# A gated recurrence and a soft mixture of experts on one core: the ninth token group as rows of seven tokens, with scans by halves of the time

## The chip, the cores and the metric

The kernel runs on one core of a Trainium2 chip. The core has five engines that run beside each other, each in the order of its own instruction list: TensorE (PE, with its weight loads shown as PEld), VectorE (DVE), ScalarE (ACT), GpSimd (POOL) and SyncE (SP, which here only issues transfers). Sixteen DMA engines move data between HBM and the core's memory. The metric is the device time of one execution in microseconds (us). PSUM is the memory that PE writes; a tile there holds its buffer until its last reader is done.

## The reference

The inputs are x and f_logit of 4 batches x 5056 steps x 256 channels in float32, a lower bound per channel, and the weights of 8 experts with 4 slots each. First a recurrence runs over the steps, then a soft mixture of experts over all 20224 tokens:

```python
f = lower_bound + (1.0 - lower_bound) * sigmoid(f_logit)
for t in range(S):
    h = f[:, t] * h + (1.0 - f[:, t]) * x[:, t]
    y[:, t] = h
logits = y @ phi                            # 20224 x 32
d = softmax of logits over the tokens;  c = softmax of logits over the slots
slot_out[e] = relu(slot_input[e] @ w1[e]) @ w2[e]     # slot_input = d.T @ y
out = c @ slot_out
```

No slot's output is known before every token has been through the recurrence, so the kernel reads all inputs first and writes all outputs last.

## The kernel before

**Tiling.** The 5056 steps of a batch are cut into ten groups. Groups 0 to 7 and 9 have 512 steps, group 8, the ninth, has the remaining 448 (`odd`, line 55). A unit is one group of one batch, so there are 40; units 32 to 35 are the ninth group of batches 0 to 3, units 36 to 39 the last group. The main loop (from line 499) runs over the units and works ahead: at unit n it loads units n+6, gates n+3 or n+4, multiplies n+3, transposes n+1 and n+2, scans n and takes n-1 on. The order of the calls in this loop is the order of instructions on each engine; nothing is reordered later, so an instruction that waits holds up all that stand behind it on its engine.

**Stages of a unit.**
- `load` (lines 215 to 236) issues the transfers of f_logit and x on SP, into tiles f_t and x_t of two units, three buffers each. Units 8 to 31 (`long`, line 198) come eight tokens a row, 8 KB; units 0 to 7 and 36 to 39 four tokens a row. The ninth group takes three DMAs for each pair of units and each of f_logit and x (lines 227 and 231): three tokens a row for 384 steps of each batch, and the last 64 steps of both batches together, one token on each partition.
- `gate` (line 246): ACT's sigmoid, s_t, for a pair of units.
- `enter` (line 257): POOL multiplies s_t and x_t to u_t.
- `s_to_channels` and `u_to_channels`: PE transposes s_t and u_t to channels by steps, into the PSUM tiles sp (one buffer, a pair of units) and up (two buffers). The ninth group (lines 266 and 269) needs one transposition for the shared last 64 steps and three more for each unit; the long units transpose 64 partitions at a time (line 282).
- `decay` (lines 310 and 317): ACT makes the decays a from sp, two instructions for a pair of units.
- `scan` (line 328): DVE runs the recurrence along the free axis, one instruction for each half of the channels, started from the last column of the batch's group before.
- `to_tokens` (line 341): PE transposes h back to tokens by channels into hp, a PSUM tile with a single buffer; `keep_tokens` (line 358) copies it to ht, by DVE for even units and by ACT for odd ones among the last.
- `logits`, `exps` (line 381, ACT), `weights_to_tokens` (lines 393 and 396, PE and a DVE copy to et) and `slots` (line 423, PE) take a whole group or two on.
- `idle` (line 194) issues matrix products whose result nobody reads, at chosen units; `BETWEEN` places some inside a transposition of units 8 and 12.

**Weights.** POOL issues 16 weight loads between its multiplications (`W_AT`, line 167; lines 147 and 157): six of them after `enter` of the last unit. The last two experts' w2 go to a tile w_t.

**The end.** The slots' experts run from line 615; PE's last products with w_t (line 714) lead to slot_out (line 749), and the output products (lines 778 and 815) and 21 MB of output follow.

The ninth group's order around its scans, for the steps below: at unit n the loop issues (decay or load), `enter`, `to_tokens(n-1)`, `s_to_channels` of the next pair at even n, `u_to_channels(n+1)`, idle products, then `scan(n)`, then `keep_tokens(n-1)`. At unit 35 the gate of 38/39 and the exp of groups 6 and 7 stand behind the decays of 36/37.

## Time and profile before

| | |
|---|---|
| median of 3 runs | 196.72 us (196.70 to 196.83) |
| the profiled execution | 196.81 us, span 195.0 us |
| mean granted PE clock over the span | 0.877 |
| busy: PE, DVE, ACT, POOL | 155.0, 147.5, 139.6, 104.8 us |
| HBM read, written | 58.23 MB, 20.71 MB |

The span is from the first instruction's start to the last one's end; the profiled execution's own time is 1.81 us longer. A line of the timeline gives the start, the duration, the engine, the source line, the operation, what is written and read with shapes, how many instructions, and in brackets how long the engine sat idle before it and what ended that. "L328" is line 328 of the kernel before. A granted clock of 1.00 is PE's full speed. The DMA share is the mean busy share of the 16 DMA engines; packets overlap, so it can come out over 1.

### The profile page before, as it was taken

Reading aid. Unit: us, or ns where it says so; the run is one execution under the profiler, and the core shown is the slowest. Engines: PE = TensorE matmul, PEld = TensorE weight load, DVE = VectorE, ACT = ScalarE, POOL = GpSimd, SP = SyncE. Lnnn points to the kernel's source line nnn. Section 1 sums busy time; section 2 is a strip of 40 time slices with the busy share of each in tenths; the row PEclk is TensorE's granted clock in tenths of the full one; section 3 lists DMA queues with packets and bytes.
Section 4 is the critical chain, followed back from the end, with each engine's and each line's share of the span. In section 5 each row is a group of like instructions: output and inputs, shape, how many; then the busy total and the mean of one; then the engine's idle time right before and its main releaser. Section 6 shows DMA issues by size and latency. Waiting matters only on the chain.

```text
span 195.0 us, 3288 instructions
## 1 busy us (share of the span) xinstructions
PE 155.0 (79%) x1206; PEld 105.7 (54%) x1206; DVE 147.5 (76%) x192; ACT 139.6 (72%) x200; POOL 104.8 (54%) x82
## 2 busy tenths in 40 slices
PE   4868888999989989788897887999899999990000
PEld 4446665776777767566675756567674433220000
DVE  2679797899799999999999999634199798770000
ACT  3688688799789999999998595634269987771000
POOL 2589568874997779884979969485030000000000
PEclk9999999999999999999999999999995555555555
DMA  6999999999999999999999999999949999999995
GB/s 202 417 423 419 428 422 427 430 423 359 381 423 425 414 323 423 430 417 317 392 422 395 273 232 213 214 213 214 184 165 426 426 440 430 430 430 430 430 430 218
DMA packets 14433, 70.75 MB, mean 363 GB/s; under 512 B 1601, under 2 KB 2882, under 8 KB 10450
## 3 DMA queue, kind: packets, MB, share of 16 engines
q1 hardware_dynamic: 11504, 62.13, 77.0%
q0 software_dynamic: 2912, 8.42, 21.8%
q8 instruction: 9, 0.15, 0.3%
q14 instruction: 6, 0.05, 0.1%
q10 hardware_dynamic: 2, 0.00, 0.0%
HBM read 58.23 MB, written 20.71 MB: 405 GB/s over the span
## 4 chain that ended last, share of the span: by engine, by line
DMA 30%; PE 21%; DVE 18%; ACT 9%; issue 6%; POOL 5%; ACTq 0%; SPq 0%; POOLq 0%; DVEq 0%
DMA x_t<-in_x_dram 15%; DVE h L328 14%; PE op L815 10%; DMA w_t<-in_moe_w_dram 9%; DMA w_sb<-in_moe_w_dram 6%; POOL u_t L257 4%; ACT oc L820 3%; DVE ht L358 3%; PE hp L341 3%; PE up L282 2%; ACT a L310 2%; PE op L778 2%; PE sp L272 2%; ACT s_t L246 1%; ACT ob L772 1%
## 5 line engine op out<-in xcount | busy, mean ns | idle before, releaser
L257 POOL TENSOR_TENSOR u_t<-s_t,x_t 128x1024 bf16<-128x1024 bf16 (+1 forms) x39 | 82.4, 2129 | 22.2 <-ACT s_t L246 14.0
L328 DVE TENSOR_TENSOR_SCAN h<-a,h,up 128x512 bf16<-128x512 f32 (+1 forms) x72 | 86.6, 1251 | 4.8 <-PE up L282 3.5
L246 ACT ACTIVATE s_t<-f_t 128x2048 bf16<-128x2048 f32 (+2 forms) x23 | 38.3, 1668 | 7.2 <-DMA f_t<-in_f_logit_dram 4.9
L341 PE MATMUL hp<-base,h 128*128 128x128 f32 (+1 forms) x160 | 28.9, 303 | 9.6 <-DVE ht L358 6.7
L341 PEld LDWEIGHTS hp<-base,h 128*128 128x128 f32 (+1 forms) x160 | 22.3, 207 | 19.4 <-DVE ht L358 11.6
L815 PE MATMUL op<-slot_bd,etall 64*128 64x512 bf16 x62 | 25.9, 582 | 0.9 <-DVE ob L768 0.2
L310 ACT ACTIVATE a<-sp,lbs 128x1024 f32<-128x1024 bf16 x24 | 25.4, 1115 | 0.6 <-PE sp L272 0.6
L820 ACT ACTIVATE oc<-op,rrow 128x256 f32<-128x256 f32 x54 | 22.1, 488 | 4.5 <-PE op L815 4.3
L823 DVE TENSOR_TENSOR oc<-op,rrow 128x512 f32<-128x512 f32 x35 | 22.3, 684 | 3.0 <-PE op L815 2.9
L194 PE MATMUL slot_ps<-base 128*128 128x256 f32 x74 | 22.7, 418 | 0.0
L272 PE MATMUL sp<-base,s_t 128*128 128x128 f32 x144 | 20.2, 281 | 3.0 <-ACT a L317 2.0
L317 ACT ACTIVATE a<-sp,lbs 128x512 f32<-128x512 bf16 (+2 forms) x22 | 17.8, 858 | 3.8 <-PE sp L272 3.5
L272 PEld LDWEIGHTS sp<-base,s_t 128*128 128x128 f32 x144 | 16.3, 144 | 6.1 <-ACT a L317 3.8
L282 PE MATMUL up<-base,u_t 64*128 64x64 f32 x192 | 17.8, 230 | 1.3 <-POOL u_t L257 1.0
L815 PEld LDWEIGHTS <-etall 64*128 64x128 bf16 x62 | 9.1, 152 | 16.6 <-issue 11.8
L282 PEld LDWEIGHTS up<-base,u_t 64*128 64x128 f32 x192 | 14.0, 138 | 6.1 <-POOL u_t L257 2.7
L358 DVE COPY ht<-hp 128x512 f32<-128x512 f32 (+1 forms) x22 | 14.7, 666 | 0.8 <-PE hp L341 0.8
L358 ACT COPY ht<-hp 128x512 f32<-128x512 f32 (+1 forms) x18 | 10.4, 580 | 6.6 <-PE hp L341 6.4
L194 PEld LDWEIGHTS slot_ps<-base 128*128 128x128 f32 x74 | 12.9, 201 | 2.5 <-issue 1.1
L328 DVE TENSOR_TENSOR_SCAN h<-a,up 128x512 bf16<-128x512 f32 x8 | 9.4, 1211 | 1.9 <-PE up L272 1.8
L372 PE MATMUL lg<-h,phi 128*32 128x512 bf16 (+1 forms) x80 | 9.6, 389 | 0.0
L272 PE MATMUL up<-base,u_t 128*128 128x128 f32 x48 | 7.9, 287 | 1.1 <-POOL u_t L257 1.0
(124 smaller groups left out, 150.4 us busy)
## 6 DMA issues: line engine op xcount, KB each, us to landing
f_t<-in_f_logit_dram SPq DMA_DIRECT2D x12, 1024.0 KB, 12.5
x_t<-in_x_dram SPq DMA_DIRECT2D x12, 1024.0 KB, 11.7
out_dram<-oc SPq DMA_DIRECT2D x6, 2048.0 KB, 13.2
w_sb<-in_moe_w_dram POOLq DMA_DIRECT2D x14, 512.0 KB, 11.1
f_t<-in_f_logit_dram SPq DMA_DIRECT2D x12, 512.0 KB, 8.4
x_t<-in_x_dram SPq DMA_DIRECT2D x12, 512.0 KB, 9.9
out_dram<-ob SPq DMA_DIRECT2D x1, 2048.0 KB, 10.1
out_dram<-oc SPq DMA_DIRECT2D x2, 896.0 KB, 6.9
```

Of the source, the lines that this page charges most:

```text
L194: nc.tensor.matmul(slot_bank[:, 1], ident_f, wide_ident, start=False, stop=False, skip_group_check=True)
L246: nc.scalar.activation(s_t, f_t, ACT.Sigmoid, scale=-1.0)
L257: nc.gpsimd.tensor_tensor(uts[n][:, :r], s_t[:, :r], x_t[:, :r], ALU.mult)
L272: nc.tensor.transpose(ps[:, :, r], t[:, r], ident_f)
L282: nc.tensor.transpose(v[:, :, r], t(r)[k].bitcast(F32), ident_f[k, k])
L310: nc.scalar.activation(a, sp[:, :, :, :, o], ACT.Identity, scale=nomlb[:, ds(o, 1)], bias=1.0)
L328: nc.vector.tensor_tensor_scan(h[:, :T, o], decays[n // 2, o][:, n % 2, :T], up[:, :T, o], hs[number(g - 1, b)][:, ds(used(g - 1) - 1, 1), ...
L341: nc.tensor.transpose(hp[:n_p, r], hw[:, :n_p, r], ident_f)
L358: copy(hts[g][:n_p, b].rearrange("p r d -> p (r d)").bitcast(F32), hps.pop(n)[:n_p].rearrange("p r c -> p (r c)"))
L815: nc.tensor.matmul(op.rearrange("p u d -> p (u d)"), ew[:, :, r], slot_bd[ds(j * 2 * NS, 2 * NS)].rearrange("s u d -> s (u d)"), start=Tru ...
L820: nc.scalar.activation(ob[:, u, r], op[:, u], ACT.Copy, scale=scale[:, r, ds(u, 1)])
L823: nc.vector.tensor_tensor(ob[:, :, r], op, scale[:, r].unsqueeze(2).broadcast_to([P, 2, D]), ALU.mult)
```

## The change

The ninth group is read as rows of seven tokens. One DMA for a pair of units and each of f_logit and x puts step 7p+r of the pair's first batch on partition 2p and of its second batch on partition 2p+1. The seven columns of a pair lie one after the other in the tile, as before four in the first unit's part and three in the second's. A unit of this group is now not a batch but a half of the time: the even unit of a pair covers steps 0 to 223 of both batches, the odd one steps 224 to 447. So `u_to_channels` takes partitions 0 to 63 or 64 to 127 of both units' u_t, seven transpositions of 64 partitions; `s_to_channels` takes seven of 128 partitions for a pair; `scan` runs four instructions of 224 columns, for two batches and two halves of the channels. Tokens of both batches follow after the odd unit's scans, and all four copies to ht are ACT's. Idle products go at units 11, 15, 17 and 36 (two there), and one of the two inside unit 12's transposition.

```diff
+    R7 = R + R3
@@ load
-                    nc.sync.dma_start(
-                        out=t[:, 0, R3],
-                        in_=src[ds(b, 2), ds(t0 + P * R3, L)].rearrange("b t d -> t b d"))
-                    for m in range(2):
-                        nc.sync.dma_start(
-                            out=t[:, m, ds(0, R3)],
-                            in_=src[b + m, ds(t0, P * R3)].rearrange("(p r) d -> p r d", r=R3))
+                        out=t.rearrange("p u r d -> p (u r d)")[:, ds(0, R7 * D)],
+                        in_=src[ds(n % B, 2), ds(first(odd), used(odd))].rearrange(
+                            "b (p r) d -> p b (r d)", r=R7))
@@ to_channels: the ninth group loses its shared transposition
+            if n // B == odd:
+                ps = ps.rearrange("c p r -> c (p r)").rearrange("c (r p) -> c p r", r=R)
+            for r in range(kept(n)):
                 nc.tensor.transpose(ps[:, :, r], t[:, r], ident_f)
-        BETWEEN = {2 * B: 3, 2 * B + 4: 2}
+        BETWEEN = {2 * B: 3, 2 * B + 4: 1}
@@ half_to_channels, now for the ninth group too
+            if n // B == odd:
+                v = ps[:, ds(0, P // 2 * R7)].rearrange("c (u p r) -> c p u r", u=2, r=R7)
@@ decay
+                sp = pss[n // 2].rearrange("c u p r -> c (u p r)").bitcast(BF16).rearrange(
+                    "c (r p u o) -> c u p r o", p=P // 2, u=2, o=DC)
+                    nc.scalar.activation(a, sp[:, :, :, ds(0, R7), o], ACT.Identity,
+                                         scale=nomlb[:, ds(o, 1)], bias=1.0)
@@ scan
+            if g == odd:
+                T //= 2
+                at = ds(n % 2 * T, T)
+                up = psus.pop(n)
+                for m in range(n - n % 2, n - n % 2 + 2):
+                    if n % 2 == 0:
+                        hs[m] = hpool.tile([P, G, DC], BF16, name="h", tag="h")
+                    for o in range(DC):
+                        last_h = (hs[m][:, ds(T - 1, 1), o] if n % 2 else
+                                  hs[number(g - 1, m % B)][:, ds(used(g - 1) - 1, 1), o])
+                        nc.vector.tensor_tensor_scan(
+                            hs[m][:, at, o], decays[n // 2, o][:, m % 2, at],
+                            up[:, ds(m % 2 * T, T), o], last_h, ALU.mult, ALU.add)
+                return
@@ keep_tokens
+            if g == odd:
+                by_scalar = True
@@ the loop, ahead of s_to_channels
-                if n != SINGLE - 2:
+                halves = (n - 1) // B == odd
+                if halves and n % 2 == 0:
+                    to_tokens(n - 2)
+                    keep_tokens(n - 2)
+                elif not halves and n != SINGLE - 2:
                     unit(to_tokens, n - 1)
@@ after u_to_channels(n + 1)
+                if halves and n % 2 == 0:
+                    to_tokens(n - 1)
-                if n in (n_unit - 5, n_unit - 4):
+                if n == n_unit - 5:
                     idle(2)
                 elif n < n_unit - 4 and n != 2 * B - 1 and (
-                        n % (2 * B) in (6, 7) and n not in (5 * B + 2, 7 * B + 2)
-                        or n <= 4 * B + 1 and n % B == 1):
+                        n % (2 * B) in (6, 7) and n not in (4 * B - 1, 5 * B + 2, 7 * B + 2)
+                        or n < 4 * B and n % B == 1):
@@ after scan(n)
-            if n not in (SINGLE - 2, n_unit - 2):
+            if n not in (SINGLE - 2, n_unit - 2) and not (n // B == odd and n % 2):
                 unit(keep_tokens, n - 1)
@@ after slots
-                if n > 2 * B and n % (2 * B) == 3:
+                if n > 3 * B and n % (2 * B) == 3:
```

More of the change, by code (lines that the diff above doesn't have):

```diff
@@ L225, in load @@
                 elif n // B == odd:
-                    b, t0 = n % B, first(odd)
                     nc.sync.dma_start(
-                        out=t[:, 0, R3],
-                        in_=src[ds(b, 2), ds(t0 + P * R3, L)].rearrange("b t d -> t b d"))
-                    for m in range(2):
-                        nc.sync.dma_start(
-                            out=t[:, m, ds(0, R3)],
-                            in_=src[b + m, ds(t0, P * R3)].rearrange("(p r) d -> p r d", r=R3))
+                        out=t.rearrange("p u r d -> p (u r d)")[:, ds(0, R7 * D)],
+                        in_=src[ds(n % B, 2), ds(first(odd), used(odd))].rearrange(
+                            "b (p r) d -> p b (r d)", r=R7))
                 else:
@@ L242, in gate @@
             if n // B == odd:
-                m = (R + R3) * D
+                m = R7 * D
                 s_t = s_t.rearrange("p u r d -> p (u r d)")[:, :m]
@@ L255, in enter, with kept, to_channels @@
             else:
-                r = R3 if n // B == odd and n % 2 else R
+                r = kept(n)
                 nc.gpsimd.tensor_tensor(uts[n][:, :r], s_t[:, :r], x_t[:, :r], ALU.mult)
-        def to_channels(n, ps, t, rest):
+        def kept(n):
+            return R3 if n // B == odd and n % 2 else R
+        def to_channels(n, ps, t):
             t = t.bitcast(F32)
             if n // B == odd:
-                flat = ps.rearrange("c p r -> c (p r)")
-                sides = ident_f.rearrange("p (t u) -> p u t", u=2)
-                v = flat[:, ds(0, P * R3)].rearrange("c (p r) -> c p r", r=R3)
-                k = P * R3 - n % 2 * L
-                nc.tensor.matmul(flat[:, ds(k, P)], rest.bitcast(F32), sides,
-                                 is_transpose=True, start=True, stop=True)
-                for r in range(R3):
-                    nc.tensor.transpose(v[:, :, r], t[:, r], ident_f)
-                return
-            for r in range(R):
+                ps = ps.rearrange("c p r -> c (p r)").rearrange("c (r p) -> c p r", r=R)
+            for r in range(kept(n)):
                 nc.tensor.transpose(ps[:, :, r], t[:, r], ident_f)
-        BETWEEN = {2 * B: 3, 2 * B + 4: 2}
+        BETWEEN = {2 * B: 3, 2 * B + 4: 1}
         def half_to_channels(n, ps, t):
             k = ds(n % 2 * (P // 2), P // 2)
-            v = ps.rearrange("c p r -> c (p r)").rearrange("c (p r) -> c p r", r=2 * R)
-            for r in range(2 * R):
+            ps = ps.rearrange("c p r -> c (p r)")
+            if n // B == odd:
+                v = ps[:, ds(0, P // 2 * R7)].rearrange("c (u p r) -> c p u r", u=2, r=R7)
+            else:
+                v = ps.rearrange("c (p r) -> c p r", r=2 * R)
+            for r in range(v.shape[-1]):
                 if r == R:
                     idle(BETWEEN.get(n, 0))
-                nc.tensor.transpose(v[:, :, r], t(r)[k].bitcast(F32), ident_f[k, k])
+                nc.tensor.transpose(v[..., r], t(r)[k].bitcast(F32), ident_f[k, k])
         def s_to_channels(n):
@@ L286, in s_to_channels @@
                 pss[n // 2] = psp.tile([P, 2, P, R], F32, name="sp", tag="sp")
-            to_channels(n, pss[n // 2][:, n % 2], sts[n // 2][:, n % 2],
-                        sts[n // 2][:, 0, R3])
+            to_channels(n, pss[n // 2][:, n % 2], sts[n // 2][:, n % 2])
         def u_to_channels(n):
             ps = psu.tile([P, P, R], F32, name="up", tag="up")
-            if long(n):
+            if long(n) or n // B == odd:
                 half_to_channels(n, ps, lambda r: uts[n - n % 2 + r // R][:, r % R])
             else:
-                to_channels(n, ps, uts[n], uts[n - n % 2][:, R3])
+                to_channels(n, ps, uts[n])
             psus[n] = ps.rearrange("c p r -> c (p r)").bitcast(BF16).rearrange(
@@ L312, in decay @@
                 return
+            if n // B == odd:
+                sp = pss[n // 2].rearrange("c u p r -> c (u p r)").bitcast(BF16).rearrange(
+                    "c (r p u o) -> c u p r o", p=P // 2, u=2, o=DC)
+                for o in os:
+                    decays[n // 2, o] = apool.tile([P, 2, G], F32, name="a", tag=f"a{o}")
+                    a = decays[n // 2, o][:, :, :T].rearrange("c u (p r) -> c u p r", r=R7)
+                    nc.scalar.activation(a, sp[:, :, :, ds(0, R7), o], ACT.Identity,
+                                         scale=nomlb[:, ds(o, 1)], bias=1.0)
+                return
             sp = sp.rearrange("c u (t o) -> c u t o", o=DC)
@@ L323, in scan @@
             T = used(g)
+            if g == odd:
[11 more added lines that the diff above has]
+                            up[:, ds(m % 2 * T, T), o], last_h, ALU.mult, ALU.add)
+                return
             h = hpool.tile([P, G, DC], BF16, name="h", tag="h")
```

## The prediction

> **What bounds the kernel now.** I read the windows by stage first, then the chain of work that ended last, then the timeline from 105 to 143 us, where the two limits meet.

> ```profile
> 90.00:100.00 10.00, 8.91 (x99) 6.73 (x99) 9.62 (x10) 9.62 (x10) 8.00 (x4) 1.00 1.04 366
> ...
> 110.00:120.00 10.00, 7.77 (x68) 6.30 (x70) 9.97 (x11) 8.94 (x10) 8.33 (x9) 1.00 1.06 235
> ...
> 130.00:140.00 10.00, 9.43 (x134) 7.02 (x131) 3.40 (x10) 4.68 (x17) 4.11 (x9) 1.00 1.08 210
> ...
> 150.00:155.00 5.00, 5.00 (x21) 2.70 (x20) 3.90 (x8) 4.92 (x14) 0.00 (x0) 0.50 1.04 427
> ```

> Columns: stretch, sum, busy us of PE, PEld, DVE, ACT, POOL, granted clock, DMA share, GB/s. The DMA share is 1 or more in all four: inputs, then weights (210 GB/s is bf16 as written; twice that is read), then the output. DVE is full to 120 us, PE after it. So two things run side by side: the DMA queue, and a chain through DVE, ACT and PE.

> ```profile
> 122.67 18.17 DMA w_t<-in_moe_w_dram
> 140.84 0.04 issue
> 140.89 0.61 PE so_ps L714 x4
> ```

> The chain of waits (start, duration, what) ends this stage at the landing of the last expert weights, 140.84. The timeline says how closely PE follows:

> ```profile
> 139.64 1.03 PE L714 MATMUL so_ps<-w_t,wide 128*128 128x256 bf16 x8 [0.39 <-DMA w_t<-in_moe_w_dram]
> ...
> 140.89 0.70 PE L714 MATMUL so_ps<-w_t,wide 128*128 128x256 bf16 x5 [0.21 <-DMA w_t<-in_moe_w_dram]
> ```

> PE waited for weights only 0.39 + 0.21 = **0.60 us**: that is all the slack of the compute chain. After it everything (slot_out, 48 us of output at about 430 GB/s) follows rigidly. Where the compute chain comes from:

> ```profile
> 109.54 0.59 ACT L358 COPY ht<-hp 112x512 f32<-112x512 f32 x1 [2.04 <-PE hp L341]
> ...
> 110.47 2.12 ACT L317 ACTIVATE a<-sp,lbs 128x1024 f32<-128x1024 bf16 x2 [0.34 <-PE sp L272]
> ...
> 112.47 1.91 ACT L246 ACTIVATE s_t<-f_t 128x2048 bf16<-128x2048 f32 x1
> ...
> 114.40 1.28 ACT L381 ACT_TABLE_LOAD   x1
> ...
> 116.71 0.58 ACT L358 COPY ht<-hp 112x512 f32<-112x512 f32 x1
> ...
> 117.34 0.75 PE L341 MATMUL hp<-base,h 128*128 128x128 f32 x4 [0.51 <-ACT ht L358]
> ...
> 119.01 0.69 DVE L396 COPY et<-ep 128x1024 bf16<-128x1024 bf16 x1
> ...
> 119.75 0.62 PE L423 MATMUL slot_ps<-ht,et 128*32 128x256 bf16 x16 [0.78 <-DVE et L396]
> ```

> hp has one PSUM buffer. The token transposes of unit 36 (117.34) waited for ACT to copy unit 35 out (116.71), which stood in ACT's queue behind the decays of 36/37 (110.47), the gate of 38/39, a table load and an exp. Behind hp(36) come ep, the et copy, the slots at 119.75, and from there to 139.25 PE and ACT hand over to each other with no other gap to give back.

> **Part 1, the loads.** Twelve DMAs (four of 128 KB in 1 KB rows, eight of 384 KB in 3 KB rows) become four of 896 KB in 7 KB rows; the bytes stay 3.67 MB. Nearest rows of the DMA view: 94 to 97 us, mostly these transfers, and 75 to 85 us, 8 KB rows:

> ```profile
> DMA packets 569, 1.23 MB, mean 410 GB/s; under 512 B 61, under 2 KB 222, under 8 KB 569
> ...
> DMA packets 581, 4.24 MB, mean 424 GB/s; under 512 B 64, under 2 KB 64, under 8 KB 64
> ```

> 3.67/0.410 - 3.67/0.424 = 8.95 - 8.66 = 0.3 us; I take **0.25**. Bounds: 0, and 0.65 if they cost as in 86 to 90 us (396 GB/s against 426). Since the queue is full, weights land 0.25 earlier. SP saves eight issues, some 3 us in its queue; the last group's loads issue earlier, but DMA is full, so that only reorders.

> **Part 2, the scans.** Eight scans of 448 become sixteen of 224, and two token copies leave DVE. The groups by shape give 1266 ns for 512 columns and 1132 for 448: 2.09 ns a column, 195 fixed, so 664 for 224, less the overlap of about 45 (four scans from 103.74 to 108.09): 0.62 each, 9.92 in all. Before: 8 x 1.08 + 2 x 0.58 = 9.80. Net +0.1. Bounds: 0.54 (half of 1.08; DVE gains 1.2) and 0.69 (the slope from starts, 1.19 against 1.08; DVE loses 1.3). I take 0.62; it follows from both durations.

> **Part 3, the new waits: the core.** A batch's h is whole only after its second half, so tokens of 32 and 33 both wait for scan(33), and those of 34 and 35 for scan(35); all four copies are now ACT's. In the order of instructions ACT runs: decays 34/35, copy 32, copy 33, decays 36/37, gate 38/39, table load, exp, copy 34, **copy 35**, decays 38/39. Before, copy 32 and 34 were DVE's.

> Scans start at 103.74 as before. The sixth ends at 107.46, the eighth at 108.70. hp(32) 107.50, copy 32 done 108.83 (0.70 + 0.58 and hand-overs). PE meanwhile does s of 36/37 (0.88 to the next, as 109.23 to 110.11), then u(35), which needs the eighth scan's buffer, to 109.36; hp(33) to 110.06; copy 33 at 110.10; decays at 110.56, against 110.47: **+0.1**. From decays to the next copy ACT is packed (110.47 to 116.71 = 6.24), so copy 34 stands at 116.80. Only then is hp free: copy 34 0.58, hp(35) 0.70, hand-overs 0.08 make **+1.36** ahead of copy 35. hp(36) goes from 117.33 to 118.78, **+1.45**. Behind it: decays 38/39 (117.17 to 118.6), u(38), ep (ends 1.63 after hp starts, 120.4), et copy 119.01 to 120.4, **+1.4**, the scans of 38 and 39 with it. DVE idles about 1 us there. If the scan takes 0.69, the eighth ends at 109.26 and 0.5 is added; at 0.54 PE's order saves only 0.25. POOL's gate wait (114.52) moves 0.1, its six weight issues (118.74) too; they have over 3 us of weights queued ahead (the one issued at 111.20 landed at 122.39), so this is free.

> **Part 4, PE.** s loses one transpose per pair; u goes from 128-row to seven 64-row transposes, all beside DVE's scans: nothing. Six of 37 idle products (0.35 each) go: units 11, 12, 15, 17 and two at 36. PE was 93 to 97% busy there, but DVE lost only 0.1 at the chain's idle of 58.20, and ACT waited for f_t at 59.10, 76.36 and 81.22, so compute cannot run ahead of the loads: 0, at best -0.4 where data allow.

> **Sum.** Compute +1.4, less slack 0.60: **+0.8**; the 0.25 that DMA gains is not seen, since PE is then last. Profiled execution 196.81 (span 195.0 and 1.81 around it) + 0.8 = 197.6; its run stood 0.09 above the median 196.72, so **197.5**. Own range 197.1 (+1.0 shift) to 198.1 (+0.5 more).

> **Rivals.** (a) Not slower: DMA stays the bound. Place: L714 on w_t. Price: -0.25, up to -0.65 with the dear loads; 196.5, down to 196.1. It decides if the compute shift is under 0.35, that is if hp(35) does not queue behind the exp, or if the early stage runs ahead. For: DMA share is over 1 throughout, and removed idles free PE. Against: one hp buffer, and ACT's order.

> (b) The clock drops. From the idle products of unit 35 (about 112) to the slots (about 121) PE would run only transposes, some 9 us; the longest such stretch before is 84.64 to 91.01, 6.4 us, at a granted clock of 1.00, and 10.05 to 16.04 likewise. For: the clock does fall to 0.50 at 147 under 64-row products, with PE 90% busy. Price: about 4.2 us of PE work from there, dearer by 582/391 (512-wide products at 0.50 and 1.00) = +2.1 at most; 199.6, nearer the forecast if the drop is short.
> [...]

> (c) It doesn't do what it says: the order of instructions shows four loads and sixteen scans, so 2% at most.

> **Chances.** Forecast 64%. (a) 22%, of which 13% below 196.33. (b) 12%. (c) 2%. A measurement tells about 0.2% (0.39) from no change: faster 0.14 ((a) below 196.33, and half of (c)), same 0.15 (196.33 to 197.11: the rest of (a) and 6% at the forecast's low edge), slower 0.71 (58% of the forecast, (b), half of (c)). Range 196.3 to 199.0: it leaves out (a) below 196.33 and the dear half of (b), 2 in 10, and takes in the bounds of scan and load.

> **What would show it.** Right: copy 34 directly behind the exp and copy 35 over 1 us later; hp(36) near 118.8; DVE idle before the last et copy; no DMA wait at L714 before slot_out. Wrong: L714 still waiting for w_t; scans of 224 off 664 ns; a clock under 1.00 before 140.

## The result, and the profile after

| | before | changed |
|---|---|---|
| median of 22 runs each | 196.98 us (196.63 to 197.38) | 199.94 us (197.09 to 203.81) |
| profiled execution | 196.81, span 195.0 | 197.97, span 196.2 |
| mean granted PE clock | 0.877 | 0.872 |

The ratio is 1.0046, 95% interval 1.0025 to 1.0067: slower. (It leaves out runs over 1.5% above the fastest of their kernel, hence its distance from that of the medians.) The kernel before spreads over 0.75 us, the changed one over 6.7. So two things want explaining: why its best run is 0.46 slower than the best before, and why most are far slower than its best.

Windows of the changed kernel, columns as in the prediction (the last three: granted clock, DMA share, GB/s):

```profile
40.00:50.00 10.00, 8.46 (x72) 6.74 (x73) 9.05 (x10) 9.94 (x10) 6.89 (x4) 0.86 1.02 379
...
110.00:120.00 10.00, 6.54 (x35) 5.36 (x34) 7.86 (x11) 8.14 (x10) 8.19 (x7) 0.83 1.07 226
...
130.00:140.00 10.00, 9.97 (x159) 7.41 (x150) 3.51 (x13) 4.33 (x16) 3.94 (x9) 1.00 1.08 210
```

DVE has fallen from 9.97 to 7.86 between 110 and 120, PE has risen to 9.97 between 130 and 140, and in two stretches the clock is under 1.00. The trace's clock records say that it was 0.50 from 47.15 to 50.57 and from 115.42 to 118.83, 3.413 us each. Over the 22 runs the time goes with the mean clock: the six runs with 0.857 or less took 200.47 to 203.81 us, the six with 0.877 or more 197.09 to 197.37. The timeline of the changed kernel:

```profile
104.22 9.24 DVE L338 TENSOR_TENSOR_SCAN h<-a,h,up 128x224 bf16<-128x224 f32 x16
...
110.77 0.59 ACT L378 COPY ht<-hp 112x512 f32<-112x512 f32 x1 [1.49 <-PE hp L359]
...
115.23 1.82 PE L264 MATMUL sp<-base,s_t 128*128 128x128 f32 x8 [1.98 <-ACT s_t L243]
...
117.50 0.58 ACT L378 COPY ht<-hp 112x512 f32<-112x512 f32 x1
...
119.14 0.59 ACT L378 COPY ht<-hp 112x512 f32<-112x512 f32 x1 [1.07 <-PE hp L359]
...
119.78 0.75 PE L359 MATMUL hp<-base,h 128*128 128x128 f32 x4 [0.68 <-ACT ht L378]
...
121.45 0.69 DVE L416 COPY et<-ep 128x1024 bf16<-128x1024 bf16 x1 [0.19 <-PE ep L413]
...
141.16 1.58 PE L740 MATMUL so_ps<-w_t,wide 128*128 128x256 bf16 x13
```

Copy 34 stands directly behind the exp, copy 35 another 1.64 later, hp(36) behind it: the queue that was forecast. Thirteen products with w_t in one run, without a bracket: no wait for weights (L740 is L714 of before). But the eight s transposes at 115.23 took 1.82, against 1.04 for the eight of units 36 and 37 at 108.49: they lie in the slow window.

### The profile page after: what moved, and what is told of

The parts are those of the page before. It is cut to its first block, busy times and chain, and to the rows that moved or that the text cites. A ratio compares the mean times of both kernels' runs of the same rounds, so it can differ in the third digit from the quotient of the medians.

```text
span 196.2 us, 3287 instructions
## 1 busy us (share of the span) xinstructions
PE 151.8 (77%) x1204; PEld 105.3 (54%) x1204; DVE 146.3 (75%) x198; ACT 140.5 (72%) x202; POOL 104.9 (53%) x82
## 4 chain that ended last, share of the span: by engine, by line
PE 36%; DVE 20%; DMA 14%; ACT 11%; issue 5%; POOL 2%; ACTq 0%; SPq 0%; DVEq 0%; POOLq 0%
DMA x_t<-in_x_dram 14%; DVE h L346 14%; PE op L841 9%; PE hp L359 6%; ACT oc L846 5%; PE up L278 4%; PE sp L264 4%; DVE ht L378 4%; PE lg L392 3%; POOL u_t L254 2%; ACT ob L798 2%; PE slot_ps L443 2%; PE so_ps L740 2%; PE tail L426 1%; DVE et L416 1%
## 5 line engine op out<-in xcount | busy, mean ns | idle before, releaser
L346 DVE TENSOR_TENSOR_SCAN h<-a,h,up 128x512 bf16<-128x512 f32 x64 | 77.8, 1265 | 7.4 <-PE up L278 4.2
L264 PE MATMUL sp<-base,s_t 128*128 128x128 f32 x158 | 23.3, 291 | 4.8 <-ACT s_t L243 2.7
L264 PEld LDWEIGHTS sp<-base,s_t 128*128 128x128 f32 x158 | 19.2, 150 | 7.9 <-ACT s_t L243 3.9
L278 PE MATMUL up<-base,u_t 64*128 64x64 f32 x220 | 20.5, 232 | 1.4 <-POOL u_t L254 1.4
L278 PEld LDWEIGHTS up<-base,u_t 64*128 64x128 f32 x220 | 16.3, 141 | 7.1 <-issue 3.0
L195 PE MATMUL slot_ps<-base 128*128 128x256 f32 x62 | 19.3, 423 | 0.0
L378 ACT COPY ht<-hp 128x512 f32<-128x512 f32 (+1 forms) x20 | 11.6, 580 | 9.7 <-PE hp L359 9.5
L321 ACT ACTIVATE a<-sp,lbs 128x512 f32<-128x512 bf16 (+1 forms) x18 | 14.0, 824 | 2.9 <-PE sp L264 2.9
L378 DVE COPY ht<-hp 128x512 f32<-128x512 f32 x20 | 13.4, 668 | 1.0 <-PE hp L359 1.0
L195 PEld LDWEIGHTS slot_ps<-base 128*128 128x128 f32 x62 | 10.9, 204 | 2.1 <-issue 0.9
## 6 DMA issues: line engine op xcount, KB each, us to landing
out_dram<-oc SPq DMA_DIRECT2D x6, 2048.0 KB, 13.8
out_dram<-ob SPq DMA_DIRECT2D x1, 2048.0 KB, 10.4
```

Source lines behind the costliest of these rows:

```text
L195: nc.tensor.matmul(slot_bank[:, 1], ident_f, wide_ident, start=False, stop=False, skip_group_check=True)
L264: nc.tensor.transpose(ps[:, :, r], t[:, r], ident_f)
L278: nc.tensor.transpose(v[..., r], t(r)[k].bitcast(F32), ident_f[k, k])
L346: nc.vector.tensor_tensor_scan(h[:, :T, o], decays[n // 2, o][:, n % 2, :T], up[:, :T, o], hs[number(g - 1, b)][:, ds(used(g - 1) - 1, 1), ...
L378: copy(hts[g][:n_p, b].rearrange("p r d -> p (r d)").bitcast(F32), hps.pop(n)[:n_p].rearrange("p r c -> p (r c)"))
```

## The experiments

To begin with, the queue (**Q**: one hp buffer and ACT's order cost a fixed amount) stood against the clock (**C**: it falls because the idle products are missing). The next theories, C', A and F, are named where they come up; A and F are about the clock and about a fetch of code.

### The removed idle products, back in four ways

`e1_idle_back` has all six back, `e6_early_idle` the four before unit 32, `e5_late_idle` the two of unit 36; `e2_before_few_idle` is the kernel before without the six. The first line pair below is in e1 and e6 (with like ones for units 11, 15 and 17), the second in e1 and e5; e2 has both the other way round.

```diff
-        BETWEEN = {2 * B: 3, 2 * B + 4: 1}
+        BETWEEN = {2 * B: 3, 2 * B + 4: 2}
@@ the loop, after u_to_channels(n + 1)
-                if n == n_unit - 5:
+                if n in (n_unit - 5, n_unit - 4):
```

> The changed kernel with all six idle products of the kernel before put back (units 11, 12, 15, 17, two at 36). Two theories share out the change's loss. Queue theory (copy 34 and copy 35 behind the exp on ACT, one hp buffer) gives a fixed loss; clock theory (the six idle products missing, the granted clock at 0.50 for some 3.3 us at 47 and again at 115 us) gives the rest and the spread of the changed kernel's times, 197.1 to 203.8 us. If both hold: clock 1.00 up to 145 us, times within 0.7 us of each other like those of the kernel before, copy 35 still over 1.5 us behind copy 34's start, hp of unit 36 at about 118.5, PE no longer waiting for w_t, 197.0 to 197.4 us. If the clock falls for another reason (the 64-row transposes of the ninth group), the drop at 115 stays. If the queue costs nothing, 196.5 us.

> The kernel before with the six idle products taken out that the change takes out, and nothing else. Clock theory: the granted clock drops to 0.50 for about 3.3 us at 47 us in a good part of the executions, and the times spread upward from 196.7 by several us, as those of the changed kernel do. If the drops need the new order of the ninth group: all times within 0.4 us of 196.8. If fewer idle products help, because PE was 93 to 97 per cent busy there: 196.4.

> The changed kernel with only the two idle products of unit 36 put back. Clock theory, with the two drops independent: none at 115 us, that at 47 us stays in part of the executions; the spread shrinks if the late drop is the dear one (it lies in the chain that ends last), to 197.0 to 198.5 us. If the early drop makes the spread, it stays at 197 to 203.

> The changed kernel with only the four early idle products put back (units 11, 12, 15, 17). Clock theory: no drop at 47 us, that at 115 us stays in part of the executions and adds about 1 us each time (PE work of 118 us at half speed, scan 37 waiting 2.1 us): 197.1 to 198.3 us. If the late drop alone made the changed kernel's spread: up to 203.

Measured: 201.14 (198.67 to 202.56; ratio 1.0185, 1.0145 to 1.0225), 197.36 (197.26 to 197.94; 1.0036, 1.0023 to 1.0049), 201.57 (197.35 to 203.12) and 201.69 (198.72 to 202.68; 1.0188, 1.0139 to 1.0238). With the idles back the changed kernel is no better; without them the profile of the kernel before keeps its clock (e2: no drop before 146). C falls: the missing idles alone are not the cause. **C'** took its place: the new order of the ninth group gives PE too little to do between 100 and 125. Windows of e1:

```profile
100.00:105.00 5.00, 3.58 (x24) 2.89 (x23) 5.00 (x7) 4.08 (x5) 4.78 (x4) 0.86 1.03 420
105.00:110.00 5.00, 5.00 (x40) 3.75 (x38) 3.65 (x7) 2.81 (x4) 3.07 (x4) 0.80 1.06 309
...
115.00:120.00 5.00, 2.77 (x17) 2.47 (x18) 3.92 (x4) 3.77 (x6) 4.00 (x2) 0.73 1.06 212
120.00:125.00 5.00, 4.22 (x24) 3.40 (x24) 1.45 (x3) 2.58 (x3) 4.81 (x9) 0.59 1.07 215
```

In the other profiles the drops lie elsewhere: e1 at 103.60 and 117.26, e5 at 103.71, e6 at 81.80, 105.70 and 122.76. All last 3.41 us or a multiple, and within one execution all lie multiples of 3.41 apart (115.42 - 47.15 = 20 x 3.413; e6's three 7.0 and 5.0 apart, e1's two 4.0). The stretches at full clock between the changed kernel's drops, and from its second drop to that of the output, are 64.85 and 34.13 us, 19 and 10 times 3.413. So the profiles look like a window of 3.413 us that runs by itself. Its phase, as the remainder of a drop's start by 3.413, was 2.8 in the profile of the changed kernel, 1.2 in e1 and 3.3 in e6.

### The copy moved, the loads alone, the waits filled

`e3_dve34`: e1 and copy 34 by VectorE. `e4_before_rows7`: the kernel before with the new loads alone; it leaves out the matching order of the ninth group's tokens, so its output is not the reference's, but the work is the same.

```diff
-                by_scalar = True
+                by_scalar = n != n_unit - 6
```

> The changed kernel with the six idles back and with one more edit: the copy of unit 34 (the first of the last two that leave TensorE's single hp buffer) is made by VectorE and not by ScalarE. Theory Q (the queue of ScalarE holds the buffer): copy 34 then runs beside the exponential and copy 35 stands directly behind the exponential, so hp(36) ends some 1.0 us earlier, measured from the end of the exponential, than in the changed kernel (there 119.78 - 117.5 = 2.3 us behind copy 34's place), and the fastest runs come to 196.6 to 196.8 instead of 197.1. Theory C' (half-clock windows of 3.4 us in 100 to 125, each worth about 1.4 us): nothing in this edit removes them, so the times go on being spread over some 196.6 to 202, with a mean granted clock below 0.88 in most runs. If Q is the whole cost the spread goes as well and all runs are within 0.3 of 196.7.

Measured: 197.91 (197.09 to 201.18; 1.0051, 1.0022 to 1.0080). Copy 35 began at 118.36, right behind the exp, and hp(36) at 118.99, 1.6 us after the exp began; in the changed kernel that was 3.3. Q's mechanism holds; the spread stays, and the fastest was not under 197.09.

> The kernel before with the new loads of the ninth token group alone (seven tokens a row, two batches in one DMA; all that computes is left as it was, so that the ninth group's tokens are taken in another order than the reference's). The load part of the forecast: DMA is done 0.25 us earlier than 140.84 and, since transfers set the end of the kernel before, the time is 196.5 (bounds 196.1 to 196.8). Theory C' (the new order of the ninth group on TensorE is what lets the clock fall): no drop of the granted clock between 100 and 125, no spread, all runs within 0.3 of 196.5. If instead the loads alone bring the spread (197 to 203), C' falls, since TensorE's list is that of the kernel before.

Measured: 196.45 (196.25 to 197.26; 0.9981, 0.9970 to 0.9992). The gain of 0.41 is clear of the noise, and no spread came with it.

`e7_filled` is e1 with idles added wherever PE stood still between units 32 and 36; `e8_filled_dve34` has the moved copy too.

```diff
+        FILL = {(n_unit - 6, 2): 1, (n_unit - 4, 0): 3, (n_unit - 4, 1): 3, (n_unit - 4, 2): 2}
@@ the loop; at three places of an even step also idle(FILL.get((n, k), 0)), k from 0 to 2
+                if n in (n_unit - 8, n_unit - 7):
+                    idle(2)
```

> The changed kernel with the idles back and with more idle matmuls put into the waits of TensorE at units 32 to 36, where it stood 1 to 2 us for the table and for copies. Theory C' (TensorE does too little in a window of some 3.4 us): clock 1.00 from 100 to 125, and the times are tight at 197.1 to 197.4, which is Q's delay alone. If the drops stay (mean clock below 0.875, times of 199 to 203), the little work of TensorE in this stretch is not what lets the clock fall. The added matmuls themselves may cost up to 0.3 us where they stand ahead of a product that could have started.

> Both remedies: the filled waits and the copy of unit 34 by VectorE. If Q and C' are both right: tight, 196.5 to 196.8, that is at or just under the kernel before (196.8). If C' is wrong: spread 196.6 to 202. If Q is wrong: tight at 197.1 to 197.4 as the filled kernel without the moved copy.

Measured: 202.07 (200.07 to 202.95; 1.0240, 1.0192 to 1.0288) and 199.71 (199.49 to 202.64; 1.0160, 1.0119 to 1.0202). A miss twice over. The profiled run of e8 has no drop before its output and still took 199.49: its idles stand in the path (et copy at 122.22, see below 119.26 without them). And e7 dropped at 81.20 and 105.09, where nothing had been filled.

### What a window counts

The records give the window's phase in each profile, so every window can be lined up with what PE did in it. In ten profiles, 377 windows at full clock lie between 6 and 143 us; eleven were followed by a drop. PE's busy time doesn't tell them apart: 1.41 to 2.62 us of 3.41 in the eleven, and over fifty others had under 2.62 and kept the clock. A weighted count does. Take 1 for a 128-row transpose, 1/4 for a 64-row one, 1.7 for a record of an idle (each idle product leaves two), 0.3 for a 32-column slots product and 1 for every other product, each by the share of its record that lies in the window. Then the eleven have 8.3 to 11.3 and all others 11.7 or more. The weights are a fit to these eleven. That they go roughly with rows x columns x streamed columns is an estimate from the shapes in the timeline: a 64-row transpose (64*128 64x64) has half the rows and half the stream of a 128-row one (128*128 128x128). (By these products an idle's record would be 2 and a slots product 0.5.)

This is theory **A**. Sliding the window along each profile from 10 to 143 us in steps of 0.1 gives the share of phases that meet a count under 11.7:

| profile | share of phases | windows that begin at |
|---|---|---|
| before | 0.26 | 77.6 to 78.4 |
| changed | 0.97 | 43.6 to 45.0, 46.2, 77.9 to 78.8, 100.3 to 101.4, 111.8 to 114.3, 116.2 to 117.0 |
| e1 | 1.00 | 77.2 to 78.0, 99.5 to 103.1, 112.5 to 113.9, 116.7 to 118.3 |

Stretches at half clock are counted as they ran, with less work done in them; without the windows that touch one, the shares of changed and e1 are 0.71 and 0.69. The change adds three poor places to the one of before: the idles of units 11 and 12 (43.6), u of the ninth group by 64-row transposes (100.3), and PE's wait for ACT (111.8). A drop at the old place, as in e6 at 81.80, makes PE some 1.5 us late (its logits at 85.05, before at 83.56); in the kernel before most of that would fit into the slack found below, an estimate, since no profile of it shows one.

### The three places guarded

`e10_guard` is e1 with one idle more at units 22 and 30, and two in step 36, ahead of the s transposes of units 38 and 39: four idle products (not three, as the expectations have it), all put into waits of PE; `e9_guard_dve34` has the moved copy too.

```diff
-                        n % (2 * B) in (6, 7) and n not in (5 * B + 2, 7 * B + 2)
+                        n % (2 * B) in (6, 7)
@@ ahead of s_to_channels
+                if n == n_unit - 4:
+                    idle(2)
                 if n % 2 == 0:
                     unit(s_to_channels, n + 2)
```

> As the guarded kernel beside it, but with the copy of unit 34 on ScalarE as in the changed kernel (that is, the changed kernel with the six idles back and three more). If A and Q are both right: no drop of the clock, a tight 196.9 to 197.4, some 0.5 above the kernel with the moved copy: that is what the queue on ScalarE costs by itself. If A is wrong: spread as with the six idles alone (198.7 to 202.6). If Q is wrong: as the kernel with the moved copy.

> The changed kernel with the six idles back, the copy of unit 34 by VectorE, and three idles more: one each at units 22 and 30, and two ahead of the s transposes of unit 36, all put where TensorE waits longer than they take. Theory A (area): TensorE's clock is kept in a free-running window of 3.413 us only if the array got about 12 whole transposes' worth of work in the window before it, work being rows x columns x streamed elements: a 128-row transpose counts 1, a 64-row one 1/4, an idle of 128x256 about 2. This was fitted to 377 windows of ten profiles, whose poorest windows begin at 77.4 to 78.4, 99.7 to 103 and 112 to 114 us; the idles are put into these three. A expects clock 1.00 up to 147, and all runs within 0.4 of 196.5, DMA-bound as the run with the new loads alone (196.45). Theory C' (activity between 105 and 119 alone matters, whatever its kind) expects the spread of 197 to 201 to stay, since nothing is added between 103 and 112.

Measured: e10 197.13 (197.01 to 197.30 in 11 runs; 1.0012, 1.0003 to 1.0021). The four idle products took the spread from 3.9 us (e1) to 0.3; no phase is left under 11.7 (the poorest window has 12.0). Windows of e10:

```profile
100.00:105.00 5.00, 4.09 (x33) 3.18 (x31) 5.00 (x7) 4.46 (x5) 4.58 (x4) 1.00 1.03 419
105.00:110.00 5.00, 5.00 (x48) 3.71 (x46) 5.00 (x10) 2.62 (x4) 4.39 (x5) 1.00 1.04 311
110.00:115.00 5.00, 3.30 (x21) 2.62 (x20) 5.00 (x8) 4.80 (x5) 3.19 (x5) 1.00 1.08 251
115.00:120.00 5.00, 3.63 (x29) 3.13 (x28) 2.96 (x4) 4.20 (x7) 5.00 (x4) 1.00 1.06 212
```

From 110 to 115 PE is busy for 3.30 us, in e1 for 3.35, yet the clock is 1.00 throughout. A foretold where the idles had to go, and the spread went; busy time, as C' had it, foretells neither this nor the drops of e7.

e9 is tight as well, but at 197.74 (197.62 to 197.95; 1.0047, 1.0033 to 1.0061), 0.61 *over* e10, though its et copy stands at 119.20 instead of 120.59. Its timeline shows where the 1.39 went:

```profile
139.35 1.03 PE L742 MATMUL so_ps<-w_t,wide 128*128 128x256 bf16 x8 [0.31 <-DMA w_t<-in_moe_w_dram]
140.61 0.70 PE L742 MATMUL so_ps<-w_t,wide 128*128 128x256 bf16 x5 [0.22 <-DMA w_t<-in_moe_w_dram]
...
142.59 0.27 PE L742 MATMUL so_ps<-w_t,wide 128*128 128x256 bf16 x1 [1.06 <-DMA w_t<-in_moe_w_dram]
```

A third wait for weights. The landings say why: of the 16 engines' shares of that piece, fifteen were in by 141.26 and one at 142.55. On queue 8, which the profile's page calls instruction, a packet of 16 KB ran from 140.54 for 1.03 us; in e10 it began at 141.41. Theory **F** takes it for PE's code, fetched as PE gets on: here PE got on sooner, and the packet came in front of one engine's last weights. The trace does not name whose code it is; the candidate below tests F.

One thing A did not foretell: e9's profile lost the clock from 39.74 to 43.15, in a place without a guard (count 11.3). The five runs lie within 0.33 us even so.

### A probe of the clock

`e11_probe` adds, behind the last work of the kernel before, stretches of one kind of PE work, with dense 128-row transposes between (`whole_rows`; `half_rows` are 64-row transposes, `narrow` products of two columns).

```diff
@@ behind the last work; between the stretches stand dense whole_rows
+        half_rows(230)
@@
+        for _ in range(115):
+            half_rows(1)
+            narrow(1)
@@
+        for _ in range(60):
+            whole_rows(1)
+            narrow(2)
@@
+        for _ in range(40):
+            whole_rows(1)
+            narrow(4)
```

> The kernel before with a probe behind its last work (about 80 us more; the outputs are made as before). Five stretches of dense 128-row transposes, between them four stretches of about 14 us: dense 64-row transposes (pitch 62 ns, 55 a window, by A 55/4 = 13.8: clock held, narrowly); 64-row transposes in turn with matmuls of two columns (about 27 a window, 6.8: clock falls to 0.50 although TensorE has no gap); 128-row transposes with two such matmuls (about 14.5: held); 128-row transposes with four (about 9.5: falls). [...]

The probe took 308.98 us. Its windows, one of each stretch in this order (the first is dense 128-row):

```profile
180.00:188.00 8.00, 8.00 (x76) 8.00 (x74) 0.00 (x0) 0.00 (x0) 0.00 (x0) 1.00 1.00 424
190.00:200.00 10.00, 10.00 (x161) 10.00 (x160) 0.00 (x0) 0.00 (x0) 0.00 (x0) 1.00 0.40 167
...
213.00:216.00 3.00, 3.00 (x21) 2.20 (x20) 0.00 (x0) 0.00 (x0) 0.00 (x0) 1.00 0.00 0
218.00:228.00 10.00, 10.00 (x49) 6.92 (x49) 0.00 (x0) 0.00 (x0) 0.00 (x0) 0.50 0.00 0
...
270.00:278.00 8.00, 8.00 (x127) 7.52 (x124) 0.00 (x0) 0.00 (x0) 0.00 (x0) 1.00 0.01 2
...
289.00:297.00 8.00, 8.00 (x166) 7.63 (x163) 0.00 (x0) 0.00 (x0) 0.00 (x0) 1.00 0.01 2
```

Dense 64-row transposes held 1.00 from 190 to 200: 161 in 10 us are 55 a window, 13.7 by A. Mixed with two-column products they lost it at 216.80 and had it back only in the dense stretch, at 261.17, with PE **busy all the time**: 3.00 of 3.00 by its records, whose ends the profile models. A pair took 0.31 us, not the 0.13 planned, so that eleven pairs fit a window and the count was about 2.7 (the two-column products taken as nothing). The last stretch missed what was expected of it by its pace: 166 records, a fifth of them transposes, make 14 a window, over the threshold, so it couldn't fall and tells nothing. Still, here PE lost the clock without a gap in its records (0.50 from 218 to 228, 10.00 of 10.00 busy), and dense transposes alone kept it (1.00 from 180 to 188).

### The candidate

`e12_few_dve34` is the changed kernel with the moved copy, the idle of unit 12 back, and the guards: five idles fewer than e9.

> The candidate: the changed kernel with the copy of unit 34 by VectorE, one of its six removed idles back (unit 12) and three guards (one idle at units 22 and 30, two ahead of the s transposes of unit 36), so five idles fewer than the guarded kernel with the moved copy (197.74). In that kernel the copy moved the weights of the last group 1.39 us ahead (120.59 to 119.20), but a 16 KB code fetch of TensorE's queue began at 140.54 instead of 141.41, on one of the 16 DMA engines, ahead of that engine's last rows of w_t (that engine's rows at 142.55 and the others' by 141.26), and TensorE waited 1.06. Theory F (fetch): five idles are 20 instructions and weight loads, about 1.1 us of TensorE's code at that place, so that the fetch begins at some 141.6, behind w_t; the last wait goes and the time is 196.3 to 196.6, that of the new loads alone (196.45), all runs within 0.4. If the fetch is not the cause (an ordering of the rows that the earlier VectorE copy brings about, say), the wait of about 1 us stays and the time with it: 197.6 to 197.9. If five idles are too few for the clock (area theory wrong), single runs at 198 and more.

Measured: **196.44** (196.32 to 196.71 in 11 runs), ratio 0.9978, 0.9969 to 0.9988: faster than both. PE stands where it stood in e9 (its product of L764 at 136.31, there 136.23), but the packet began at 142.00 and the third wait is gone, as F had it:

```profile
119.26 0.69 DVE L416 COPY et<-ep 128x1024 bf16<-128x1024 bf16 x1
...
140.50 0.71 PE L742 MATMUL so_ps<-w_t,wide 128*128 128x256 bf16 x5 [0.20 <-DMA w_t<-in_moe_w_dram]
141.05 0.27 PE L752 MATMUL tail<-w_t,gain 128*128 128x256 bf16 x1
```

## Why the prediction was right, and where it was wrong

The sign was right, and 197.5 lies by the ratio (1.0046 x 196.72 = 197.6) and by the profiled run (197.97). That nearness is luck: with the clock held up, in e10, the change makes +0.27, not the +0.8 of the sum, and the rest goes with drops of the clock, which the forecast put at nothing. By them the median of all runs, 199.94, lies outside the range; a clock under 1.00 before 140, which the forecast named as a sign of being wrong, did come. The pieces, by runs beside the kernel before (196.84 to 196.86 there): the loads -0.41 (e4); the scans by halves nothing more (e12 equals e4); copy 34 on ACT, together with five idles, +0.69 (e10 over e12; e10 and e9, which differ in the copy alone, come out the other way, by the packet of theory F); a clock without guards 0 to +6.7, +2.8 at the median (changed kernel over e10, each on its own chip; before stood at 196.98 and 196.86 there).

**Part 1, the loads.** -0.25 was forecast, -0.41 measured, within the bounds. "Not seen" was right for the changed kernel, as PE is last there.

**Part 2, the scans.** Sized wrong, without effect: sixteen take 9.24, 0.58 each, not 0.62 and 9.92. Each lasts 649 ns, close to the 664 of the forecast; it's the overlap that was 0.07 and not 0.045. The forecast's own bound of 0.54 was as near. DVE's gain of 0.68 isn't seen, because the next copy waits for PE (1.49 at 110.77).

**Part 3, the queue.** Right to two tenths where the clock stayed up: in e10 copy 34 stands at 116.91 (116.80 was forecast), copy 35 1.37 behind it (1.36), hp(36) at 118.94 (118.78) and the et copy at 120.59 (120.4), 1.58 later than before. e10 against e12, which differ in copy 34 and five idles, have 120.59 and 119.26, +1.33, and e10 against e9 +1.39. In the changed kernel's own profile, with its two drops, the et copy is at 121.45.

**The sum, "less slack 0.60".** This step failed. In e10, whose clock stayed up, the delay of the product at 136.18 (before) to 137.64 is 1.46, and the time only +0.27. I had taken the slack from two brackets. The timeline of before has a third wait without one:

```profile
136.77 0.53 PE L406 MATMUL tail<-ones,etall 128*128 128x128 bf16 x5
137.39 1.03 PE L714 MATMUL so_ps<-w_sb,wide 128*128 128x256 bf16 x8
```

In e10 the same two stand closer:

```profile
138.22 0.52 PE L426 MATMUL tail<-ones,etall 128*128 128x128 bf16 x5
138.59 1.04 PE L742 MATMUL so_ps<-w_sb,wide 128*128 128x256 bf16 x8
```

The next product starts 0.62 after these five before, and 0.37 after them in e10: 0.25 of waiting, for weights whose last landing is at 137.35. And the run of products broken by waits was dearer in itself: thirteen took 1.58 in one piece (e10), 1.03 + 0.70 in two (before); there and at the hand-over at 139.08 some 0.3 goes. 0.60 + 0.25 + 0.30 = 1.15, and 1.46 - 1.15 = 0.31, against 0.27 measured.

**Part 4 and rival (b), the clock.** Part 4 costed the removed idles at nothing, and looked only at what they delay, not at what they hold up. Of the three new places only that at 43.6 comes from the idles; those at 100 and 112 stay in e1, with all six back, and so come from the new order. Rival (b) had the right suspicion (12%), a place that is one of three, and a price too low: +2.1 "at most", where single runs paid up to 6.7. Against it stood two stretches of transposes alone that had held 1.00 (10.05 to 16.04 and 84.64 to 91.01). They had, but by A's count no window in them holds under 13.7. Sparser windows hold less: the two before the drops of the changed kernel's profile, from 43.73 and from 111.99, in which PE was busy for 2.28 and 1.44 us, have 10.9 and 10.4. By A, whether an execution pays is a matter of phase: the same kernel took 197.09 to 203.81. That transposes as such let the clock fall was not shown: the probe's dense ones held 1.00 (128-row 180 to 188, 64-row 190 to 200). Nor did the probe's drop at 216.80 have a gap in PE's records before it (3.00 of 3.00 busy from 213 to 216).

**Rival (a)** did not come, because compute was last; e12 shows what it would have been, 196.44 against the 196.5 forecast for it.

**Open.** Why no run of e3 came under 197.09, though by the count about one phase in ten meets no poor window: a packet of queue 8 in front of the last weights, as in e9, would do it, but no profile of such a run was taken. (The profile of e3, 197.19, has a drop at 104.00 and its thirteen products in one run.) And the 0.5 us of e2: there the second output's issue took 1.17 us on SP instead of some 0.4, and DMA ran short for 0.6 us; what held the issue wasn't tried.

## What to carry to other kernels

Before idle products are removed, or transposes cut into smaller ones, count what work PE gets in every window of 3.4 us (here up to 11.3 by A's count lost the clock, and 11.7 or more kept it), not how long PE is busy; one profile shows one phase, so slide the window over it, and look at the spread of the times first. Read the slack of a chain at every hand-over, also where no bracket stands. And when a chain gets shorter, look at what now collides: the same edit that took 1.4 us off the path (e9) brought a packet of queue 8, 1.03 us long, in front of one engine's last weights.
